# Seven block products for part of the first matmul in the last five passes of an attention and feed-forward kernel, with a re-ordered start

## Chip, cores, metric

One core of a Trainium2 chip. The metric is device time in microseconds, from runs of the whole program. The engines are PE (matmuls), PEld (its weight loads), DVE (vector), ACT (scalar), POOL, and SP, which issues most transfers (all but two in the trace of before).

## The reference, cut

```python
# per batch of 8, head of 8; seq 576, head_dim 64
q_s = softmax over head_dim of q;  k_s = softmax over seq of k
x = q_s @ (k_s.T @ v)                      # heads side by side: (8, 576, 512)
xn = (x - mean) / sqrt(var + 1e-6) * g_ln
out = x + relu(xn @ w_ch1) @ w_ch2         # 512 -> 2048 -> 512
```

The kernel works in nine passes: eight with 512 tokens of one batch each, and a ninth with the 64 tokens left of each batch. g_ln and the mean are worked into w1 ("centring"); the division by the deviation comes at the end.

## The kernel before: the parts concerned

The kernel is a list of tasks, each with an engine, an estimated duration, what it reads and writes, and a priority class. A small simulation of the engines at build time puts them into one fixed order per engine; at run time each engine works through its list strictly in that order. An order that rests on a transfer that lands later than estimated makes the engine stand (DVE for 0.87 us, up to 22.35 us, in the trace of before).

The first matmul of a pass makes 16 blocks of 128 hidden units from four blocks of x:

```python
for n, m in enumerate(order):                        # 16 blocks
    for ko in range(k0, KO1):                        # 4 matmuls 512 wide
        nc.tensor.matmul(bank[gi], w1_sb[:, ko, m*P:m*P+P], xt[:, ko], ...)
    relu_evac(m, bank[gi], (bk, gi), eng(n))         # PSUM -> fp16 hT
    if split and n in (HK, KO2 - 1):
        sums(0 if n == HK else 4)                    # sums of hT for the second matmul
```

Cutting both operands of a matmul into 2 x 2 blocks gives eight block products; with sums and differences of blocks as operands, seven are enough, an eighth fewer multiplications for some additions (in the trace of before an undisturbed matmul of a pass took 12.23 us in seven products and 13.81 us plain). The second matmul was already in seven block products, save in the first pass. DVE makes the sums that this needs (`S` of hT, `T` of w2) and adds up the products as they come out of PSUM (`cp`, `ot`).

The start loads w1 in four column blocks, converts each on ACT or DVE, takes its column mean through a matmul with a matrix of ones, and subtracts it on DVE:

```python
on_act = ((1,), (0, 1, 3), (1,), (1, 3))[blk]
...
after = state["kve"] if blk == 1 and (kp or ko not in on_act) else ()
if blk == 2:
    after = (state["nm"],) if ko in on_act else state["ev"][1]
```

The attention of a later batch goes beside the matmuls: loads of q, k and v; exponentials on ACT (`eq`, `ek`); copy of v to fp16 (`vb`); key-value products (PE, evicted as `kve`); a transposition of `eq` by DMA; and the x products, evicted on ACT to `xsT`, which the next first matmul reads.

The softmax here doesn't subtract the row's maximum and nothing guards it: scores larger than these inputs give would overflow.

## Time and profile before

| | before |
|---|---|
| median of 3 timed runs | 279.06 us (278.26 to 279.4) |
| profiled run, span | 277.7 us, 275.9 us |
| first matmuls of batch 1, 2 and 4 start at (PE timeline) | 52.25, 80.10, 135.89 us |
| end of PE's last matmul | 272.08 us |

The page of the profile gives busy time and the chain of work that ended last, followed back from the end. The timeline lists instructions in time, with the idle time ahead of them and what ended it in brackets. "Stretches" give length, then busy time of PE, PEld, DVE, ACT and POOL with instruction counts, then the granted PE clock, the DMA share (in this view it can exceed 1) and GB/s. The prediction shows the lines of before.

### The profile page before, as it was taken

To read this page: it belongs to the slowest core of one execution; us is meant where nothing else is said; L and a number is where in the kernel's file an instruction comes from. 1 tells how busy PE (TensorE), PEld (TensorE's weight loads), DVE (VectorE), ACT (ScalarE), POOL (GpSimd) and SP (SyncE) were. 2 spreads that over 40 slices of the span, in tenths; PEclk is the share of its full clock that TensorE was granted. 3 is DMA by queue.
4 is the path that set the end of the run, shared out by engine and by line. 5 is a ranking of instruction groups with operands and counts; after the bars stand their busy time and mean duration, and the time that the engine had idled before them with its cause. 6 is when DMAs were issued, how large, how long until landed. Compare 5 with 4: busy or idle time off the path is not lost.

```text
span 275.9 us, 5670 instructions
## 1 busy us (share of the span) xinstructions
PE 268.4 (97%) x2324; PEld 163.7 (59%) x2324; DVE 198.5 (72%) x412; ACT 168.2 (61%) x274; POOL 1.7 (1%) x12
## 2 busy tenths in 40 slices
PE   8988999999999999999999999999999999999994
PEld 3433445446864587458745874578457845874583
DVE  1788998998769767966697669766976764742562
ACT  4678966788598693659466856685664076016500
POOL 2000000000000000000000000000000000000000
PEclk9999999999999999999999999999999999999999
DMA  7999999799989994499659965796544450022004
GB/s 257 361 386 387 388 388 233 184 330 256 319 265 187 280 334 48 143 216 389 75 153 185 395 100 154 160 394 124 154 86 77 78 154 0 0 64 90 1 4 152
DMA packets 55874, 54.83 MB, mean 199 GB/s; under 512 B 34596, under 2 KB 35112, under 8 KB 55848
## 3 DMA queue, kind: packets, MB, share of 16 engines
q1 hardware_dynamic: 55696, 54.34, 69.6%
q8 instruction: 18, 0.29, 0.4%
q10 hardware_dynamic: 152, 0.13, 0.1%
q14 instruction: 8, 0.07, 0.1%
HBM read 36.70 MB, written 9.44 MB: 167 GB/s over the span
## 4 chain that ended last, share of the span: by engine, by line
PE 91%; DMA 4%; SPq 1%; ACT 1%; DVE 1%; issue 0%
PE pg L575 43%; PE pg L654 35%; PE pg L717 5%; DMA stg<-in_v_dram 4%; PE pa L391 2%; PE pa L422 2%; PE pa L654 1%; PE pa L575 1%; SPq L238 1%; PE pa L288 1%; PE pg L553 1%; ACT hT L538 1%; PE pa L445 0%; PE pa L519 0%; DVE vb L377 0%; ACT w_sb L271 0%
## 5 line engine op out<-in xcount | busy, mean ns | idle before, releaser
L538 ACT ACTIVATE hT<-pg 128x512 f16<-128x512 f32 x134 | 78.8, 598 | 65.2 <-PE pg L575 64.8
L575 PE MATMUL pg<-xsT,w_sb 128*128 128x512 f16 x488 | 108.4, 379 | 0.8 <-ACT hT L538 0.8
L575 PEld LDWEIGHTS <-w_sb 128*128 128x128 f16 x568 | 54.8, 98 | 65.9 <-DVE w_sb L294 1.6
L654 PEld LDWEIGHTS <-S 128*128 128x128 f16 x512 | 49.6, 98 | 6.3 <-issue 0.4
L654 PE MATMUL pg<-T,S 128*128 128x256 f16 x368 | 41.9, 273 | 0.0
L654 PEld LDWEIGHTS <-hT 128*128 128x128 f16 x384 | 37.2, 98 | 7.8 <-issue 2.2
L591 DVE TENSOR_TENSOR S<-hT 128x1024 f16<-128x1024 f16 x32 | 21.8, 681 | 26.5 <-ACT hT L538 26.5
L664 DVE SCALAR_TENSOR_TENSOR cp<-pg,st,x 128x256 f32<-128x256 f32 x46 | 20.2, 479 | 14.2 <-PE pg L654 13.7
L664 DVE SCALAR_TENSOR_TENSOR ot<-pg,st,cp 128x256 f32<-128x256 f32 x47 | 20.5, 477 | 12.2 <-PE pg L654 12.0
L654 PE MATMUL pg<-w_sb,hT 128*128 128x256 f16 x248 | 29.2, 273 | 0.0
L527 DVE BATCH_NORM_STATS2 bst<-x 128x6 f32<-128x512 f16 x36 | 23.9, 666 | 4.8 <-DMA x<-xsT 4.8
L342 DVE TENSOR_REDUCE zq<-eq 128x18 f32<-128x1152 bf16 x16 | 21.5, 1344 | 4.7 <-ACT eq L340 4.7
L340 ACT ACTIVATE eq<-stg 128x1152 bf16<-128x1152 f32 x16 | 18.7, 1170 | 7.3 <-DMA stg<-in_q_dram 7.2
L346 DVE TENSOR_TENSOR eq<-eq,rzq 128x1152 bf16<-128x1152 bf16 x16 | 21.6, 1352 | 0.3
L370 ACT ACTIVATE ek<-stg 128x1152 bf16<-128x1152 f32 x16 | 18.7, 1170 | 3.0 <-DMA stg<-in_k_dram 3.0
L380 ACT CAST vb<-stg 128x1152 f16<-128x1152 f32 x15 | 17.6, 1174 | 4.4 <-DMA stg<-in_v_dram 4.3
L435 ACT CAST xsT<-pa 128x512 f16<-128x512 f32 x31 | 16.0, 592 | 3.0 <-PE pa L422 3.0
L654 PE MATMUL pg<-w_sb,S 128*128 128x256 f16 x128 | 15.3, 273 | 0.0
L717 PE MATMUL pg<-w_sb,hT 128*128 128x512 f16 x64 | 14.8, 380 | 0.0
L654 PE MATMUL pg<-T,hT 128*128 128x256 f16 x120 | 14.4, 273 | 0.0
L575 PE MATMUL pg<-xT,w_sb 128*128 128x512 f16 x64 | 14.0, 379 | 0.0
L740 PE MATMUL pg<-zero 128*128 128x512 f16 x33 | 10.6, 481 | 1.2 <-DVE zero L223 1.2
(71 smaller groups left out, 162.6 us busy)
## 6 DMA issues: line engine op xcount, KB each, us to landing
stg<-in_q_dram SPq DMA_DIRECT2D x16, 576.0 KB, 5.3
stg<-in_k_dram SPq DMA_DIRECT2D x16, 576.0 KB, 7.2
stg<-in_v_dram SPq DMA_DIRECT2D x16, 576.0 KB, 9.0
out_dram<-ot SPq DMA_DIRECT2D x33, 256.0 KB, 3.7
stg<-in_moe_w_ch_dram SPq DMA_DIRECT2D x16, 512.0 KB, 10.8
out_dram<-ot SPq DMA_DIRECT2D x1, 512.0 KB, 2.8
out_dram<-ot SPq DMA_DIRECT2D x1, 128.0 KB, 2.7
out_dram<-ot ACTq DMA_DIRECT2D x1, 128.0 KB, 2.2
```

Source lines behind the costliest of these rows:

```text
L340: plan.add("ACT", act_t(QW), lambda: nc.scalar.activation(e.rearrange("p j (s d) -> p s j d", s=2), sv(s), AF.Exp), r=sk(s), w=[("eq", u, ...
L342: plan.add("DVE", dve_t(QW), lambda: nc.vector.reduce_sum(zq[:, hf], eh, axis=AX.X), r=[("eq", u, hf)], w=[("zq", hf)], cls=qcls, after=sums_)
L346: plan.add("DVE", dve_t(QW), lambda: nc.vector.tensor_tensor(eh, eh, rzq[:, hf].to_broadcast([P, 2 * JT, D]), op=ALU.mult), r=[("rzq", hf) ...
L370: plan.add("ACT", act_t(QW), lambda: nc.scalar.activation(ek[u][:, hf].rearrange("p j (s d) -> p s j d", s=2), sv(s), AF.Exp), r=sk(s), w= ...
L380: plan.add("ACT", act_t(QW), lambda: nc.scalar.copy(vd, va), r=sk(s), w=[("vb", u, hf, i) for i in range(2)], cls=cls, slack=late, after=t ...
L527: plan.add("DVE", dve_t(512), lambda j=j: nc.vector.bn_stats(bst[:, j, :], x[:, j, :]), r=[(xk, j)], w=[("bst", j)], cls=cls, slack=2.0 if ...
L538: nc.scalar.activation(hT[:, m, :], bank, AF.Relu)
L575: nc.tensor.matmul(bank[gi], w1_sb[:, ko, m * P : m * P + P], xt[:, ko], start=(ko == 0), stop=(ko == KO1 - 1))
L591: plan.add("DVE", dve_t(256 * n, 2), lambda: nc.vector.tensor_tensor(S[i][:, ks], a, b, op=op), r=r, w=sk(i), cls=0.3 if k0 else 0.45)
L654: nc.tensor.matmul(g[i][0], fa(k, i), fb(k), start=(first and k == 0 and (i == 0 or g[0][1] != g[1][1])), stop=(last and k == HK - 1), ski ...
L664: nc.vector.scalar_tensor_tensor(dst[:, i, :], in0=g[i][0], scalar=sti[:, 4, 2 * t0 + i : 2 * t0 + i + 1], in1=src[:, i, :], op0=ALU.mult, ...
L717: nc.tensor.matmul(pg[gis[j]], hT[:, kk, j * P : j * P + P], w2_sb[:, kk, :], start=(kk == 0), stop=(kk == KO2 - 1))
```

## The change

Its intent: the first matmul too in seven block products, for as many row groups of w1 as the other engines can carry, one in batches 4 to 6 and two in batch 7 and the ninth pass; a start whose order fits the landing of its loads; and v rows 66 wide instead of 65, so that each starts on 4 bytes. Cut to its core:

```diff
-    vb = [sb([P, 2, JT, 2, VW], FP16, f"vb{i}") for i in range(2)]
+    vb = [sb([P, 2, JT, 2, VW + 1], FP16, f"vb{i}") for i in range(2)]
-        on_act = ((1,), (0, 1, 3), (1,), (1, 3))[blk]
+        on_act = ((0, 1), (0, 1), (1,), (1, 3))[blk]
-                after = state["kve"] if blk == 1 and (kp or ko not in on_act) else ()
+                after = state["kve"] if blk == 1 and ko else ()
-                    after = (state["nm"],) if ko in on_act else state["ev"][1]
+                    after = (state["nm"],) if ko in on_act else (state["subs"],) if kp else state["ev"][1]
+        for k0, k1 in ((0, 2), (2, 4)) if blk == 0 else ((0, 4),):   # centring in two halves
-            queries(1, lq, kves[:1])
+            queries(1, lq, kves)
-            keys(1, lk)
+            keys(1, lk, (state["nm"],))
 ... (load estimates, slack, keys of hT by half)
+    UNITS = {c: (1,) for c in (4, 5, 6)}
+    UNITS[7] = UNITS[8] = (0, 1)
+    def w1_sums(n, before): ...      # 4 DVE sums of w1 quarters -> WS[n]
+    def x_sums(c): ...               # 4 DVE differences of x quarters -> TX
+            def product(self, a, b, g, first, last): ...   # 4 matmuls 256 wide
+            def copy(self, g, n): ...                      # ACT: PSUM -> fp32 SBUF
+            def end(self, g, m0, t, n=None): ...           # ACT ReLU, or DVE add + max
+            u.product("11", "11", 0, True, False);  u.copy(0, 0)
+            u.product("12", "21", 1, True, True);   u.end(1, 0, 0, 0)
+            u.product("S2", "T2", 0, False, False); u.copy(0, 1)
+            u.product("S1", "T1", 2, True, False);  u.copy(2, 2)
+            u.product("S3", "T3", 0, False, False); u.end(0, HK, 1, 2)
+            u.product("S4", "22", 2, False, True);  u.end(2, 0, 1, 1)
+            u.product("22", "T4", 0, False, True);  u.end(0, HK, 0)
```

More of the change, by code (lines that the diff above doesn't have):

```diff
@@ L260, in load_w1 @@
             load(stg[s][:, :1024].rearrange("p (a n) -> p a n", a=2),
-                 w1_src[:, 2 * kp : 2 * kp + 2, blk * 512 : blk * 512 + 512], sk(s), 0.524 if blk or kp else 0.72)
+                 w1_src[:, 2 * kp : 2 * kp + 2, blk * 512 : blk * 512 + 512], sk(s), 0.524 + (0.4 if (blk, kp) == (2, 0) else 0))
             for a in range(2):
                 ko = 2 * kp + a
-                after = state["kve"] if blk == 1 and (kp or ko not in on_act) else ()
+                after = state["kve"] if blk == 1 and ko else ()
                 if blk == 2:
-                    after = (state["nm"],) if ko in on_act else state["ev"][1]
+                    after = (state["nm"],) if ko in on_act else (state["subs"],) if kp else state["ev"][1]
                 dst = w1_sb[:, ko, blk * 512 : blk * 512 + 512]
@@ L285, in centre_w1, with f @@
         wk = [("w1", blk, ko) for ko in range(KO1)]
-        def f():
-            for ko in range(KO1):
-                nc.tensor.matmul(bank, ones, w1_sb[:, ko, cs], start=(ko == 0), stop=(ko == KO1 - 1))
-        plan.add("PE", 0.216 * KO1, f, r=wk + ["ones"], w=[bk], cls=0)
+        for k0, k1 in ((0, 2), (2, 4)) if blk == 0 else ((0, 4),):
+            def f(k0=k0, k1=k1):
+                for ko in range(k0, k1):
+                    nc.tensor.matmul(bank, ones, w1_sb[:, ko, cs], start=(ko == 0), stop=(ko == KO1 - 1))
+            plan.add("PE", 0.216 * (k1 - k0), f, r=wk[k0:k1] + ["ones"], w=[bk], cls=0)
         state["nm"] = plan.add("ACT", act_t(512), lambda: nc.scalar.copy(nm, bank), r=[bk], w=["nm"], cls=-0.5)
@@ L302, in centre_w1 @@
         sub(0, 4, 0, 1)
-        sub(0, 4, 1, 4)
+        state["subs"] = sub(0, 4, 1, 4)
     def load_w2(k0, eng="DVE"):
@@ L367, in pe_t_evac, with keys @@
             plan.add("ACT", act_t(128), lambda: nc.scalar.copy(et[:, hf, 8], v16[1][:, 0]), r=[("pa", tb[1])], w=[("eqT", u, 2)], cls=0)
-        def keys(hf, s):
+        def keys(hf, s, exps=exps):
             plan.add("ACT", act_t(QW), lambda: nc.scalar.activation(
@@ L391, in f @@
                                 nc.tensor.matmul(pa[ab[n][e]][c0 : c0 + D, :VW], ek[u][r0 : r0 + R, hf, j, c0 : c0 + D],
-                                                 vb[u][r0 : r0 + R, hf, j, i, :], start=(j == 0), stop=(j == JT - 1))
+                                                 vb[u][r0 : r0 + R, hf, j, i, :VW], start=(j == 0), stop=(j == JT - 1))
             ids = []
@@ L395, in kv @@
             plan.add("PE", 0.1 + 0.42 * len(hs), f, r=[("ek", u, h) for h in hs] + [("vb", u, h, i) for h in hs for i in range(2)],
-                     w=[("pa", a) for x in ab for a in x], cls=0, slack=SLACK if steady else 0.2, after=kvs)
+                     w=[("pa", a) for x in ab for a in x], cls=0, slack=SLACK if steady else 0.2 if b else 0.0, after=kvs)
             for n, h in enumerate(hs):
@@ L456, in attn @@
         if kind == "first":
-            lq, lk, lv = [load_half(b, t, 0, x) for t, x in ((q, 0), (k, 0), (v, 0))]
+            lq, lk, lv = [load_half(b, t, 0, x) for t, x in ((q, 0), (k, 0), (v, 0.2))]
             queries(0, lq)
@@ L541, in relu_evac @@
         if eng == "ACT":
-            plan.add("ACT", act_t(512), fa, r=[bk], w=[("hT", m)], cls=0)
+            plan.add("ACT", act_t(512), fa, r=[bk], w=[("hT", m, 0), ("hT", m, 1)], cls=0)
         else:
-            plan.add("DVE", dve_t(512), fd, r=[bk], w=[("hT", m)], cls=0)
+            plan.add("DVE", dve_t(512), fd, r=[bk], w=[("hT", m, 0), ("hT", m, 1)], cls=0)
     def mm1_open(gis):
@@ L580, in mm1, with sums @@
         return ids
-    def sums(k0):
+    def sums(k0, seven=False):
         n = 4
@@ L587, in sums @@
         h12, h22 = hT[:, kh, 0:256], hT[:, kh, 256:512]
-        lo, hi = [("hT", k0 + i) for i in range(n)], [("hT", HK + k0 + i) for i in range(n)]
+        lo, hi = [[("hT", k + i, t) for i in range(n) for t in range(2)] for k in (k0, HK + k0)]
         sk = lambda i: [("S", i, k0 + j) for j in range(n)]
         def tt(i, a, b, op, r):
-            plan.add("DVE", dve_t(256 * n, 2), lambda: nc.vector.tensor_tensor(S[i][:, ks], a, b, op=op), r=r, w=sk(i), cls=0.3 if k0 else 0.45)
+            plan.add("DVE", dve_t(256 * n, 2), lambda: nc.vector.tensor_tensor(S[i][:, ks], a, b, op=op), r=r, w=sk(i),
+                     cls=(-0.25 if i < 2 else -0.1) if seven else 0.3 if k0 else 0.45)
         tt(0, h21, h22, ALU.add, lo + hi)
@@ L634, in mm2_split @@
         rk = lambda t0: [(stk, "r", 2 * t0), (stk, "r", 2 * t0 + 1)]
-        hk = lambda k0: [("hT", k0 + k) for k in range(HK)]
+        hk = lambda k0, t: [("hT", k0 + k, t) for k in range(HK)]
         skey = lambda i: [("S", i, k) for k in range(HK)]
@@ L639, in mm2_split @@
         h = lambda k, t0, i: hT[:, k, 256 * t0 + i * P : 256 * t0 + i * P + P]
-        A = {"11": (lambda k, i: h(k, 0, i), hk(0)), "12": (lambda k, i: h(HK + k, 0, i), hk(HK)),
-             "22": (lambda k, i: h(HK + k, 1, i), hk(HK))}
+        A = {"11": (lambda k, i: h(k, 0, i), hk(0, 0)), "12": (lambda k, i: h(HK + k, 0, i), hk(HK, 0)),
+             "22": (lambda k, i: h(HK + k, 1, i), hk(HK, 1))}
         for i in range(4):
@@ L647, in mm2_split, with product @@
             Bm[f"T{i + 1}"] = ((lambda k, i=i: T[i][:, k, :]), tkey(i))
-        def product(a, b, g, first, last):
+        def product(a, b, g, first, last, after=()):
             (fa, ka), (fb, kb) = A[a], Bm[b]
@@ L656, in f @@
                                          skip_group_check=True)
-                plan.add("PE", 0.1093 * len(ks), f, r=[ka[k] for k in ks] + [kb[k] for k in ks], w=[g[i][1]])
+                n = plan.add("PE", 0.1093 * len(ks), f, r=[ka[k] for k in ks] + [kb[k] for k in ks], w=[g[i][1]], after=after)
+            return n
         gk = lambda g: [g[0][1], g[1][1]] if g[0][1] != g[1][1] else [g[0][1]]
@@ L686, in mm2_split @@
         add_x(2, gb, 1, 256)
-        product("S3", "T3", ga, False, False)
+        n = product("S3", "T3", ga, False, False)
         state["stats"] = (final(o2, 1, ga, 2, 1),)
@@ L691, in mm2_split @@
                      r=[("ot", o2, 1)], mb=0.26, land=2.0, cls=0)
-        product("S4", "22", gb, False, True)
+        product("S4", "22", gb, False, True, (n,) if c == B else ())
         final(o1, 1, gb, 1, 0)
@@ L718, in f @@
                                          start=(kk == 0), stop=(kk == KO2 - 1))
-                i = plan.add("PE", 0.864, f, r=[("hT", kk) for kk in range(k0, k0 + 4)] + [("w2", kk) for kk in range(k0, k0 + 4)], w=[("pg", gis[j])])
+                i = plan.add("PE", 0.864, f, r=[("hT", kk, t) for kk in range(k0, k0 + 4) for t in range(2)] + [("w2", kk) for kk in range(k0, k0 + 4)], w=[("pg", gis[j])])
                 if j == 0:
@@ L744, in warm, with w1_sums, tt @@
         return plan.add("PE", 0.43 * n, lambda: zeros(pg[3], True)(n), r=["zero"], w=[("pg", 3)], cls=0)
+    UNITS = {c: (1,) for c in (4, 5, 6)}
+    UNITS[7] = UNITS[8] = (0, 1)
+    WS = [ek[0].bitcast(FP16).rearrange("p a j c -> p (a j c)")[:, :2048].rearrange("p (i k n) -> p i k n", i=4, k=2),
+          sb([P, 4, 2, 256], FP16, "WS1")]
+    WSK = [[("ek", 0, 0), ("ek", 0, 1)], []]
+    def w1_sums(n, before):
+        lo, hi = slice(256 * n, 256 * n + 256), slice(1024 + 256 * n, 1024 + 256 * n + 256)
+        a11, a12, a21, a22 = w1_sb[:, 0:2, lo], w1_sb[:, 2:4, lo], w1_sb[:, 0:2, hi], w1_sb[:, 2:4, hi]
+        def tt(i, a, b, op, r=()):
+            plan.add("DVE", dve_t(512, 2), lambda: nc.vector.tensor_tensor(WS[n][:, i], a, b, op=op),
+                     r=list(r) + [("w1c", m0 + 2 * n + j, k) for m0 in (0, HK) for j in range(2) for k in range(2)], w=WSK[n] + [("WS", n, i)], cls=0.8, after=before)
+        tt(0, a21, a22, ALU.add)
+        tt(1, WS[n][:, 0], a11, ALU.subtract, [("WS", n, 0)])
+        tt(3, a12, WS[n][:, 1], ALU.subtract, [("WS", n, 1)])
+        tt(2, a11, a21, ALU.subtract)
@@ new lines, in x_parts @@
+    def x_parts(c):
+        xt = (xsT[c % 2] if c < B else xT8).rearrange("p (j k) t -> p k j t", j=J)
+        xkeys = XK(c % 2) if c < B else [("xT8", b, i) for b in range(B) for i in range(2)]
+        if c < B - 1:
+            return xt, xkeys, x8.rearrange("p j (k n) -> p j k n", k=2), [("x8", j) for j in range(J)]
+        tx = ek[1].bitcast(FP16).rearrange("p a j c -> p (a j c)")[:, :2048].rearrange("p (i k n) -> p i k n", i=4, k=2)
+        return xt, xkeys, tx, [("ek", 1, 0), ("ek", 1, 1)]
@@ new lines, in x_sums, with tt @@
+    def x_sums(c):
+        xt, xkeys, TX, tk = x_parts(c)
+        b11, b12, b21, b22 = [xt[:, 2 * k : 2 * k + 2, 2 * t : 2 * t + 2, :] for k in range(2) for t in range(2)]
+        T4 = lambda i: TX[:, i].rearrange("p k (j t) -> p k j t", j=2)
+        def tt(i, a, b, r=()):
+            plan.add("DVE", dve_t(512, 2), lambda: nc.vector.tensor_tensor(T4(i), a, b, op=ALU.subtract),
+                     r=xkeys + list(r), w=tk + [("TX", i)], cls=0.2)
+        tt(0, b12, b11)
+        tt(1, b22, T4(0), [("TX", 0)])
+        tt(2, b22, b12)
+        tt(3, b21, T4(1), [("TX", 1)])
@@ new lines, in mm1_seven, with __init__, product, f @@
+    def mm1_seven(c):
+        last = c >= B - 1
+        units = UNITS[c]
+        xt, xkeys, TX, tk = x_parts(c)
+        bufs = [(t, (n, i)) for n, ts in (("pg", pg), ("pa", pa)) for i, t in enumerate(ts)]
+        raw = lambda k0, m0: (lambda n, k, m: w1_sb[:, k0 + k, (m0 + 2 * n + m) * P : (m0 + 2 * n + m) * P + P])
+        A = {"11": raw(0, 0), "12": raw(2, 0), "22": raw(2, HK)}
+        for i in range(4):
+            A[f"S{i + 1}"] = lambda n, k, m, i=i: WS[n][:, i, k, m * P : m * P + P]
+        Bm = {"11": (lambda k: xt[:, k, 0:2, :], xkeys), "21": (lambda k: xt[:, 2 + k, 0:2, :], xkeys),
+              "22": (lambda k: xt[:, 2 + k, 2:4, :], xkeys)}
+        for i in range(4):
+            Bm[f"T{i + 1}"] = ((lambda k, i=i: TX[:, i, k, :]), [("TX", i)])
+        ids = []
+        class Unit:
+            def __init__(self, n):
+                self.n = n
+                if last:
+                    self.g = [bufs[(3 * n + i) % 8] for i in range(3)]
+                    self.cp = [(stg[3 * n + i][:, :512], sk(3 * n + i)) for i in range(3)]
+                else:
+                    self.g = [(pa[i], ("pa", i)) for i in [nxt("pa", 4) for _ in range(3)]]
+                    self.cp = [(cp[i], [("cp", i)]) for i in range(3)]
+            def product(self, a, b, g, first, last):
+                fa, (fb, kb) = A[a], Bm[b]
+                bank, bk = self.g[g]
+                def f():
+                    for i in range(2):
+                        for k in range(2):
+                            nc.tensor.matmul(bank[:, 256 * i : 256 * i + 256], fa(self.n, k, i), fb(k),
+                                             start=(first and i == 0 and k == 0), stop=(last and k == 1), skip_group_check=True)
+                ids.append(plan.add("PE", 0.437, f, r=kb + ([("WS", self.n, int(a[1]) - 1)] if a[0] == "S" else []), w=[bk]))
+            def copy(self, g, n):
+                bank, bk = self.g[g]
+                plan.add("ACT", act_t(512), lambda: nc.scalar.copy(self.cp[n][0], bank), r=[bk], w=self.cp[n][1], cls=-0.3)
+            def end(self, g, m0, t, n=None):
+                bank, bk = self.g[g]
+                bank = bank.rearrange("p (i n) -> p i n", i=2)
+                m = m0 + 2 * self.n
+                h = hT[:, m : m + 2, 256 * t : 256 * t + 256]
+                w = [("hT", m, t), ("hT", m + 1, t)]
+                if n is None:
+                    plan.add("ACT", act_t(512), lambda: nc.scalar.activation(h, bank, AF.Relu), r=[bk], w=w, cls=-0.2)
+                    return
+                cp_, ck = self.cp[n]
+                plan.add("DVE", dve_t(512), lambda: nc.vector.tensor_tensor(h, bank, cp_.rearrange("p (i n) -> p i n", i=2), op=ALU.add),
+                         r=[bk] + ck, w=w, cls=-0.3)
+                if t == 0 or not last:
+                    plan.add("DVE", dve_t(512, 4), lambda: nc.vector.tensor_scalar_max(h, in0=h, scalar1=0.0), r=w, w=w, cls=-0.2)
+                else:
+                    plan.add("ACT", act_t(512), lambda: nc.scalar.activation(h, h, AF.Relu), r=w, w=w, cls=-0.1)
+        def direct(m):
+            if last and m >= HK:
+                gi = nxt("pa", 4)
+                bank, bk = pa[gi], ("pa", gi)
+            else:
+                gi = nxt("pg", 4)
+                bank, bk = pg[gi], ("pg", gi)
+            def f():
+                for ko in range(KO1):
+                    nc.tensor.matmul(bank, w1_sb[:, ko, m * P : m * P + P], xt[:, ko], start=(ko == 0), stop=(ko == KO1 - 1))
+            ids.append(plan.add("PE", 0.864, f, r=xkeys, w=[bk]))
+            relu_evac(m, bank, bk, "ACT")
+        for n0 in (0, 2):
+            for n in (n0, n0 + 1):
+                for m in [m0 + 2 * n + i for i in range(2) for m0 in (0, HK)] if n not in units else ():
+                    direct(m)
+            us = [Unit(n) for n in (n0, n0 + 1) if n in units]
+            for u in us:
+                u.product("11", "11", 0, True, False)
+                u.copy(0, 0)
+                u.product("12", "21", 1, True, True)
+                u.end(1, 0, 0, 0)
+            for u in us:
+                u.product("S2", "T2", 0, False, False)
+                u.copy(0, 1)
+                u.product("S1", "T1", 2, True, False)
+                u.copy(2, 2)
+            for u in us:
+                u.product("S3", "T3", 0, False, False)
+                u.end(0, HK, 1, 2)
+                u.product("S4", "22", 2, False, True)
+                u.end(2, 0, 1, 1)
+            for u in us:
+                u.product("22", "T4", 0, False, True)
+                u.end(0, HK, 0)
+            sums(2 * n0, last)
+        return ids
@@ L777 @@
             state["tok"] = tokens(b, 0.7 if b > 1 else 0.35, stats=state["stats"])
+        rstd = state.get("rstd")
+        if b == min(UNITS) - 1:
+            w1_sums(1, before)
+        if b == B - 2:
+            w1_sums(0, before)
+        if b in UNITS:
+            x_sums(b)
+        ids = mm1_seven(b) if b in UNITS else mm1(b, b > 0, () if b else opened)
         if b == B - 1:
-            tokens(8, 0.7, stats=state["stats"])
-        rstd = state.get("rstd")
-        ids = mm1(b, b > 0, () if b else opened)
+            tokens(8, 0.9, stats=state["stats"])
+            x_sums(8)
         if b == 0:
@@ L794 @@
         before = (ids[-1], rstd)
-    mm1(8, True)
+    mm1_seven(8)
     mm2_split(8)
```

## The prediction

> **What bounds the kernel now.** I read the head of the page first, then the chain of work that ended last in order of time, then the stretches between the starts of its stages, then the groups. On the page:
>
> ```profile
> span 275.9 us, 5670 instructions
> PE 268.4 (97%) x2324; PEld 163.7 (59%) x2324; DVE 198.5 (72%) x412; ACT 168.2 (61%) x274; POOL 1.7 (1%) x12
> PE 91%; DMA 4%; SPq 1%; ACT 1%; DVE 1%; issue 0%
> ```
>
> PE is 97% busy, and, which says more, 91% of the chain that set the end is PE, mostly one matmul behind another (line 575 is the first matmul, 654 the second one, already in seven block products). The chain in order of time gives the stage lengths:
>
> ```profile
> 20.49 0.59 ACT cp L290
> 21.07 0.64 ACT w_sb L271
> 21.71 1.47 ACT hT L538 x3
> 23.18 0.04 issue
> 23.23 1.90 PE pg L575 x8
> ...
> 219.95 13.81 PE pg L575 x64
> 233.76 12.23 PE pg L654 x112
> 245.99 13.81 PE pg L575 x64
> ```
>
> An undisturbed first matmul is 13.81 us for 64 matmuls 512 wide, 215.8 ns each. An undisturbed second one is 12.23 us for 112 matmuls 256 wide, 109.2 ns each. From 23.23 us on the chain hardly leaves PE. So matmul time taken away there is time saved, if nothing new makes PE wait. Ahead of 23.23 us there are a DMA wait and a hole. The timeline of DVE in the hole:
>
> ```profile
> 20.99 0.49 DVE L274 TENSOR_SCALAR w_sb<-stg,g_sb 128x512 f16<-128x512 f32 x1 [0.67 <-DMA stg<-in_moe_w_ch_dram]
> 22.35 0.49 DVE L274 TENSOR_SCALAR w_sb<-stg,g_sb 128x512 f16<-128x512 f32 x1 [0.87 <-DMA stg<-in_moe_w_ch_dram]
> 22.75 1.28 DVE L294 TENSOR_TENSOR w_sb<-w_sb,cp 128x512 f16<-128x512 f16 x2
> ```
>
> The subtraction that releases column block 1 of w1 (line 294, at 22.75) has had its operand since ACT wrote it at 21.08, but in DVE's fixed order it stands behind two conversions of block 2 whose transfers had not landed. PE began its next matmuls at 23.23. That is an ordering fault, and the diff aims at it.
>
> Room on the other engines, one row per batch (batches 3 to 8, the last with the tail):
>
> ```profile
> 108.19:136.05 27.86, 27.86 (x266) 18.00 (x264) 20.44 (x44) 18.78 (x30) 0.00 (x0) 1.00 0.81 206
> 136.05:164.03 27.98, 27.98 (x265) 17.97 (x264) 20.86 (x45) 18.77 (x30) 0.00 (x0) 1.00 0.79 205
> 164.03:192.09 28.06, 28.02 (x266) 18.00 (x264) 21.30 (x46) 18.78 (x30) 0.00 (x0) 1.00 0.74 205
> 192.09:219.95 27.86, 27.86 (x266) 17.98 (x264) 22.05 (x49) 12.32 (x24) 0.00 (x0) 1.00 0.45 98
> 219.95:245.99 26.04, 26.04 (x178) 17.23 (x176) 15.43 (x34) 10.11 (x20) 0.00 (x0) 1.00 0.15 42
> 245.99:275.90 29.91, 26.08 (x177) 17.03 (x174) 12.62 (x24) 9.54 (x16) 0.00 (x0) 1.00 0.23 71
> ```
>
> After the length come busy PE, weight loads, DVE, ACT, POOL. PE fills every batch; DVE has 6 to 7 us free in batches 4 to 6 and 10 or more in the last two; the clock is full.
>
> [...] seven products instead of eight keep nearly all of their 12.5%. [...] (a 512-element sum for w2 took 414 to 416 ns, a 1024-element one 690) and for PSUM (a 512-element eviction took 682 ns)[...]. [...] The v rows are 65 fp16 wide, 130 bytes[...]; the cast into them took 753 ns for 576 elements[...], where the aligned fp32-to-fp16 cast of w2 took 690 ns for 1024[...]. [...] whether 66-wide rows help is open.
>
> **The change part by part.**
>
> *Matmuls.* A row group is four blocks of 128 hidden units. Plain, it takes 4 x 4 = 16 matmuls of 512: 13.81 / 4 = 3.45 us. In seven products of 2 x 2 matmuls of 256 it takes 28 x 109.2 ns = 3.06 us. Saved 0.39 us. There is one such group in each of batches 4, 5 and 6 and two in each of passes 7 and 8 (the last pass is that of the ninth tokens): seven groups, 7 x 0.395 = 2.8 us, all of it on the PE chain. Weight loads rise from 16 to 28 a group at 98 ns each, under the 109 ns spacing, as in the second matmul now.
>
> *ACT.* A plain group has four evictions of 0.60 us. The new one has three copies and one ReLU of the same 512 elements: the same 2.4 us. In the last two passes two ReLUs a group are added; ACT has over 15 us free there.
>
> *DVE.* A group gets three additions from PSUM (0.68 us each, as the eviction row) and three maxima on fp16 [...], 2.9 us; in the last two passes only one maximum, 2.3 us. Each such pass needs four differences of x (4 x 0.41 = 1.7 us, done in the batch before), and each group once four sums of w1 (1.7 us, in batches 3 and 6). New DVE sums: batch 3, 20.4 + 3.3 = 23.7 of 27.9; batch 4, 20.9 + 4.6 = 25.5 of 27.6; batch 5, 21.3 + 4.6 = 25.9 of 27.7; batch 6, 22.1 + 4.6 + 1.7 = 28.4 of 27.5, so nearly 1 us must move to its neighbours; batch 7, 15.4 + 4.6 + 1.7 = 21.7 of 25.2; the last, 12.6 + 4.6 = 17.2. It fits, at 92 to 100% in three batches.
>
> *PSUM and order.* Within one group a product that adds to a bank must wait for the copy out of it: about 0.6 us and a hand-over, against 0.44 us of the product between. The plan can put plain matmuls of another group there, and in the last passes two groups alternate. I charge 0.05 to 0.1 us a group, 0.4 us in all, for waits that the plan's model misses.
>
> *Start.* Conversions of w1 move between ACT and DVE (block 0 to ACT, block 1 to DVE), the first value product is no longer parted by a conversion waiting on a transfer, the centring of block 0 opens after two of its four matmuls' data, and the late half of block 2 is put behind the subtraction of block 1. The clear part is the hole: the subtraction takes about 0.42 us for its first part, so from 21.08 PE could begin near 21.6 to 22.3 instead of 23.23: 0.9 to 1.6 us. The cast of v may lose another 0.3 us ahead of the first matmul at 17.24, but ACT's own half of v ends at 16.56, so little of that counts. Against it: DMA is busy at 98% or more from 17 to 80 us, so what waits for transfers there cannot move up, and ACT, which works in order, evicted x for batch 2 only at 78.74, behind a key conversion whose load landed at 77.67; the first matmul of batch 2 at 80.17 started just as that eviction went on. I let 0.9 us come through.
>
> Sum: 2.8 - 0.4 + 0.9 = 3.3 us, so 279.06 - 3.3 = 275.8 us.
>
> **Rivals.** *DVE becomes the bound in batches 4 to 6.* For it: the sums above, and that DVE worked without a break over the first 13 us of batch 4, just where the new additions fall. They push the query normalisation, its transpose and the x products later by up to 3 us. Against it: x products of batch 5 began at 151.73 and are needed at 164.03, and the first 10 us of slack take this in. If it wins, PE waits 0.5 to 1 us in each of three batches and the result is 277 to 278 us. *The start gain is hidden by transfers.* For it the DMA shares; against it, PE runs unbroken from 23.23 on and the waits there are of order. If it wins fully, 276.7 us. *The start gain comes whole*, 1.6 us, and the plan's waits are nil: 274.7 us. *The groups' waits for PSUM copies are not filled*: up to 0.4 us at two places in each of seven groups, 5 us, which would turn the change into a loss of 2 us less the start gain; the plan sees these waits and has other matmuls ready, so I give it little.
>
> **Range and chances.** 274.5 to 277.3 us holds most of this. Over 2% faster would be under 273.5, 5.6 us, which needs twice the matmul saving or a start gain that no row above shows: 5%. Slower by 2% needs the unfilled waits and a lost start together: 1%. Within 2%: 94%.
>
> **What would show it.** The chain of the profile after should have first matmuls of 13.4 us of PE time in batches 4 to 6 and 13.0 in the last two, with no DVE or ACT pieces in it; the stretches should show DVE near 25.5 us in batches 4 and 5; PE's idle time after 25 us should stay below 1 us; the first matmuls after the hole should start near 22.3; and the v cast should show 753 ns or about 450. I am wrong if DVE releases PE again and again in batches 4 to 7, if matmuls 256 wide with w1 as weights come at over 115 ns, or if the start of batch 1 (52.41) does not move up by 0.5 to 1.5 us.

In the sums for DVE the ground of one term is: a group's 2.9 us (2.3 in the last two passes) are three additions of 0.68 us, as the eviction of 682 ns, and 0.9 us for three maxima (0.3 for one). The trace of before has no such maximum; in the changed kernel one took 287 ns (line 841). That seven products keep nearly all of their eighth is in the chain: 28 x 109.2 ns against 16 x 215.8 ns is 11.4% less. What wider v rows would give no trace had shown. The 0.3 us, and the "about 450" ns at the end, can stand only as an estimate: 576 elements on the line through the sums' 415 ns for 512 and 690 for 1024, which is also what the cast of w2 took for 1024, make 0.45 us.

## The result and the profile after

275.25 us, median of 4 runs (274.09 to 275.85), beside 278.96 us for before: faster, by less than 2%. The ratio is 0.9864 (95% interval 0.9825 to 0.9904). A ratio is the mean time of one kernel's fast runs over that of the other's of the same rounds, so not quite the ratio of these medians. Predicted were 275.8 us and a gain of 3.3 us; measured were 3.7. Line numbers move: 854 and 819 are the plain and the seven-product matmuls of the new routine, 576 the old first matmul, 656 the second.

The head of the page of the kernel after, and its chain by engine:

```profile
span 273.1 us, 5912 instructions
PE 264.3 (97%) x2403; PEld 171.3 (63%) x2403; DVE 224.0 (82%) x474; ACT 169.6 (62%) x282; POOL 1.7 (1%) x12
PE 74%; DMA 15%; DVE 4%; ACT 3%; SPq 2%; issue 2%
```

PE busy fell by 4.1 us, partly because fewer filler matmuls run in the start (28 instead of 33). DVE rose by 25.5 us and PE stayed at 97%. The chain now leaves PE more often: DMA has 15% of it, against 4%. That is where to look for the start. The share is not lost time: PE's named waits after 25 us sum to 0.85 us (0.41, 0.23 and 0.21), but at each of them the chain goes back to the work that released PE. The groups of the new work (line, engine, operation, output and inputs, count, busy us, mean ns, idle before):

```profile
L838 DVE TENSOR_TENSOR hT<-pa,cp 128x512 f16<-128x512 f32 x9 | 5.9, 682 | 0.0
L841 DVE TENSOR_SCALAR hT<-hT 128x512 f16<-128x512 f16 x13 | 3.5, 287 | 0.2
L825 ACT COPY cp<-pa 128x512 f32<-128x512 f32 x9 | 5.0, 586 | 0.2 <-PE pa L819 0.2
L378 DVE CAST vb<-stg 128x576 f16<-128x576 f32 x1 | 0.8, 754 | 0.0
```

The additions took 682 ns each, as the prediction has them, and the maxima 287 ns: 3 x 0.682 + 3 x 0.287 = 2.9 us a group, the prediction's sum. The v cast on DVE took 754 ns, 753 before: the wider rows did nothing for it. PE's timeline in batch 4 holds the one wait of the new routine:

```profile
141.93 0.60 PE L819 MATMUL pa<-xsT,WS 128*128 128x256 f16 x4
142.36 1.03 PE L854 MATMUL pg<-xsT,w_sb 128*128 128x512 f16 x4
...
145.76 0.60 PE L819 MATMUL pa<-x,w_sb 128*128 128x256 f16 x4 [0.21 <-DVE hT L838]
```

The next row starts 0.43 to 0.44 us after four matmuls 256 wide (141.93 to 142.36): 109 ns each, as expected. Plain matmuls stand between the products of the group, so that the copies out of PSUM are hidden. Only the seventh product waited, 0.21 us, for a DVE addition.

The stretches of 27.6, 27.6 and 27.4 us from the start of batch 4:

```profile
136.00:163.60 27.60, 27.39 (x272) 18.58 (x271) 24.92 (x55) 17.08 (x30) 0.00 (x0) 1.00 0.76 208
163.60:191.20 27.60, 27.60 (x274) 18.73 (x272) 25.01 (x54) 19.48 (x34) 0.00 (x0) 1.00 0.81 208
191.20:218.60 27.40, 27.40 (x279) 19.30 (x278) 24.22 (x56) 13.30 (x25) 0.00 (x0) 1.00 0.47 99
```

DVE is at 88 to 91%, PE has next to no gap. PE's first row of batch 4 and its last row, before:

```profile
135.89 9.78 PE L575 MATMUL pg<-xsT,w_sb 128*128 128x512 f16 x44
...
271.04 1.04 PE L654 MATMUL pa<-T,hT 128*128 128x256 f16 x8
```

and after:

```profile
135.83 3.65 PE L854 MATMUL pg<-xsT,w_sb 128*128 128x512 f16 x16
...
268.25 1.04 PE L656 MATMUL pa<-T,hT 128*128 128x256 f16 x8
```

From the first matmul of batch 4 to PE's end (start and length of the last row) the kernel before took 272.08 - 135.89 = 136.19 us, this one 269.29 - 135.83 = 133.46 us: 2.73 us less, for seven groups at an expected 0.395, 2.77.

The start is another story. The old hole is gone, but a new one stands at block 2. DVE in the kernel after:

```profile
26.29 0.69 DVE L311 CAST w_sb<-stg 128x1024 f16<-128x1024 f32 x1 [0.87 <-DMA stg<-in_moe_w_ch_dram]
27.02 0.43 DVE L607 TENSOR_TENSOR T<-w_sb 128x512 f16<-128x512 f16 x1
27.36 1.29 DVE L295 TENSOR_TENSOR w_sb<-w_sb,cp 128x512 f16<-128x512 f16 x2
```

A conversion of w2 stands ahead of the subtraction, waiting for its load; PE waited 0.41 us for the subtraction. The first matmul of batch 1 still began 0.58 us earlier (51.67 instead of 52.25), but that of batch 2 only 0.13 us earlier (79.97 instead of 80.10). The chain in order of time shows the loss:

```profile
69.72 7.88 DMA stg<-in_k_dram
...
77.62 0.03 ACT ek L371
77.64 1.04 issue
78.69 1.06 ACT xsT L436 x2
...
79.79 0.25 PE pa L446 x6
80.04 9.73 PE pg L576 x44
```

ACT evicts x for batch 2 only after a key exponential of batch 3 whose load landed at 77.6. So I had two theories to test. P: the products are the whole gain, and the start gain is lost again ahead of batch 2 by an engine's fixed order. S: about 1 us of the start does come through, which would explain why the timed runs differ by 3.7 us where the trace shows 2.8 (span 275.9 to 273.1). Later ones: T, full DMA queues hand every gain of the start back; and D, DVE is about to become the bound.

### The profile page after: what moved, and what is told of

Read it like the earlier page. It is cut to its first block, busy times and chain, and to the rows that moved or that the text cites. A ratio compares the mean times of both kernels' runs of the same rounds, so it can differ in the third digit from the quotient of the medians.

```text
span 273.1 us, 5912 instructions
## 1 busy us (share of the span) xinstructions
PE 264.3 (97%) x2403; PEld 171.3 (63%) x2403; DVE 224.0 (82%) x474; ACT 169.6 (62%) x282; POOL 1.7 (1%) x12
## 4 chain that ended last, share of the span: by engine, by line
PE 74%; DMA 15%; DVE 4%; ACT 3%; SPq 2%; issue 2%
PE pg L656 26%; PE pg L576 15%; PE pg L854 11%; DMA stg<-in_moe_w_ch_dram 7%; PE pg L720 5%; PE pg L819 4%; PE pa L819 3%; DMA stg<-in_k_dram 3%; DMA x<-xsT 3%; PE pa L854 3%; DMA stg<-in_v_dram 2%; PE pa L392 2%; SPq L238 1%; PE pa L576 1%; PE pa L656 1%
## 5 line engine op out<-in xcount | busy, mean ns | idle before, releaser
L539 ACT ACTIVATE hT<-pg 128x512 f16<-128x512 f32 x98 | 57.8, 599 | 34.2 <-PE pg L854 20.6
L576 PE MATMUL pg<-xsT,w_sb 128*128 128x512 f16 x232 | 51.9, 379 | 0.4 <-DVE w_sb L295 0.4
L656 PE MATMUL pg<-T,S 128*128 128x256 f16 x368 | 43.5, 273 | 0.0
L576 PEld LDWEIGHTS <-w_sb 128*128 128x128 f16 x248 | 23.7, 98 | 29.3 <-DVE w_sb L295 1.2
L854 PE MATMUL pg<-xsT,w_sb 128*128 128x512 f16 x160 | 38.3, 379 | 0.0
L854 PEld LDWEIGHTS <-w_sb 128*128 128x128 f16 x208 | 20.0, 98 | 17.6 <-issue 0.2
```

What stands on the lines that cost most here:

```text
L539: nc.scalar.activation(hT[:, m, :], bank, AF.Relu)
L576: nc.tensor.matmul(bank[gi], w1_sb[:, ko, m * P : m * P + P], xt[:, ko], start=(ko == 0), stop=(ko == KO1 - 1))
L656: nc.tensor.matmul(g[i][0], fa(k, i), fb(k), start=(first and k == 0 and (i == 0 or g[0][1] != g[1][1])), stop=(last and k == HK - 1), ski ...
L854: nc.tensor.matmul(bank, w1_sb[:, ko, m * P : m * P + P], xt[:, ko], start=(ko == 0), stop=(ko == KO1 - 1))
```

## The experiments

Twelve runs follow, the first of the changed kernel itself. Each edit reaches the chip through the plan, which can move other instructions too: PE's list is that of the changed kernel in e3, e4b, e5b and e10; in e4, e8 and e9 it changed with the edit, in e1, e2 and e7 it must. In the table, starts come from PE's timeline of the one profiled run, times from 6 runs. Where a kernel's own profile and its timed runs differ, it is because the same kernel's runs spread by 1 to 3 us. e0, e1, e2 and e4, and later e8 to e10, ran on one chip, e4b, e5b, e6 and e3 on a second, e7 on a third; each group beside runs of the kernel before.

### e0: the changed kernel again

> The changed kernel once more, unaltered, as the yardstick for the runs beside it and for a second trace. Its first trace puts batches 4 to the end 2.7 us under before (what the seven groups should give) and the start of batch 2 only 0.1 us earlier, yet the timed runs differed by 3.7 us. Theory P (the products are the whole gain, the start gain is swallowed in batch 1): 2.6 to 3.0 us under before. Rival S (about 1 us of the start does come through in the timed runs): 3.5 to 4.0 us under before.

Measured: 274.43 us against 278.01, ratio 0.9876 (0.984 to 0.9912). Batch 1 starts at 51.30, batch 2 at 79.82, batch 4 to the end takes 133.04 us. The timed difference, 3.5 us, lies where S begins; the interval (2.4 to 4.4 us) holds both theories.

### e1: the products with the old start

The edit takes back every hunk of the start and of the v rows, for instance:

```diff
-        on_act = ((0, 1), (0, 1), (1,), (1, 3))[blk]
+        on_act = ((1,), (0, 1, 3), (1,), (1, 3))[blk]
-            queries(1, lq, kves)
+            queries(1, lq, kves[:1])
```

> The seven products with the old start: all edits of the loading and centring of w1, of the first attention and of the v rows taken back. Theory P: 2.6 to 3.0 us under before, within 0.3 us of the changed kernel. Rival S: only the 2.7 us of the matmuls remain and the changed kernel is about 1 us faster than this.

Measured: 275.30 us, ratio 0.9896 (0.9865 to 0.9927), so 2.9 us under before. From batch 4 to the end 133.50 us, as with the changed kernel. Theory P's number. The difference from e0, 0.6 us in the means, is within the noise.

### e2: the start without the products

The same hunks put onto the old kernel, with the padded rows.

> The old kernel with the new start and the padded v rows, without the seven products. Theory P: within 0.3 us of before, with mm1 of batch 1 starting some 0.7 us earlier and mm1 of batch 2 at the old time, held by ACT, which stands behind a key load that has not landed. Rival S: about 1 us under before.

Measured: 277.93 us against 278.01, ratio 1.0003 (0.9966 to 1.004): nothing; S's 1 us lies at the interval's edge (0.34%, 0.9 us). In the profile, batch 1 starts at 51.41, 0.84 us earlier, and batch 2 at 81.01, later than before; from batch 4 to the end 136.20 us, as before (136.19). ACT stood at the query load of batch 3 until 74.17, in front of an eviction that PE waited for.

### e4: keys behind the evictions of x

```diff
-                r=sk(s), w=[("ek", u, hf)], cls=cls, slack=late, after=exps)
+                r=sk(s), w=[("ek", u, hf)], cls=cls, slack=late,
+                after=tuple(exps) + (tuple(state["ev"][-1]) if b == 3 else ()))
```

> The changed kernel with one order edge added: the two key exponentials of batch 3 on ACT go behind the four evictions of x of batch 2. If the start gain is lost because those evictions wait behind a key load (theory P), the first matmul of batch 2 begins at 79.4 to 79.6 us instead of 80.04 and the whole is 0.4 to 0.6 us faster than the changed kernel. If the transfers themselves are the bound there (rival T: everything in that stretch is held by the full DMA queues), the wait turns up elsewhere, in the value products of batch 3 or the next transposition, and nothing is gained.

Measured: 275.73 us, ratio 0.9912 (0.9883 to 0.9942), 1.1 us slower in the means than e0. Batch 2 starts at 79.45, 27.89 us after batch 1: without a gap, as theory P wanted. But the plan moved the value products of batch 3 from 89.70 to 92.50 us, and PE waited 0.57, 0.47 and 0.27 us between 97 and 103 us. P's account of the loss is right, its forecast of a gain was wrong.

### e4b: only the second keys behind them

The same edge with `b == 3 and hf`; PE's order is that of the changed kernel.

> The changed kernel; of batch 3 only the second key exponential goes behind the four evictions of x of batch 2, PE's order stays as it was. The last run moved both keys: its batch 2 started at 79.4 us without a gap, but the value products of batch 3 then went 3 us later and PE waited 1.3 us in that batch. If the loss of the start gain is ACT's order and not the transfers (theory P), this starts the first matmul of batch 2 at 79.3 to 79.6 us, keeps the value products of batch 3 near 89.2 us, and is 0.3 to 0.6 us faster than the changed kernel. If the transfers hold that stretch (rival T), batch 2 starts early but PE waits again before batch 4 and the time stays within 0.2 us of the changed kernel.

Measured: 275.16 us, ratio 0.9896 (0.9869 to 0.9922). Batch 2 starts at 79.83, again with no gap after batch 1 (51.97), and no wait follows before batch 4. But the start itself was 0.3 us later in this run, and the time is no better. Against an interval of 0.3%, a gain of 0.3 to 0.6 us can't be confirmed.

### e5b: that, and w2's first conversion behind the subtraction

```diff
-            r=sk(s), w=[("w2", k0), ("w2", k0 + 1)])
+            r=sk(s), w=[("w2", k0), ("w2", k0 + 1)], after=(state["subs2"],) if k0 == 0 else ())
```

> The edge of the run before, and the first conversion of w2 on DVE put behind the subtraction of column block 2 of w1, so that DVE no longer stands at a w2 load in front of it (0.87 us of idle time, 0.4 us of it passed on to PE in the changed kernel at 27.8 us). Theory P: the wait at 27.8 us goes, the first matmul of batch 1 starts 0.3 to 0.5 us earlier, and 0.2 to 0.5 us of it comes through: 0.6 to 1.0 us faster than the changed kernel, the fastest so far. Rival T: batch 2 starts when its transfers let it, no faster than the run before.

Measured: 274.83 us, ratio 0.9887 (0.9861 to 0.9913), the same as e4b; theory P's 0.6 to 1.0 us under the changed kernel did not come. The wait at 27.8 us is gone and batch 1 starts at 51.42. Then ACT stood at the first query load of batch 3 until 73.84, PE waited 0.53 us for the eviction behind it, and batch 2 started at 80.21. The gain of the start was taken away at the same place by another load.

### e6: two groups in batch 6 (a failed experiment)

```diff
-    UNITS[7] = UNITS[8] = (0, 1)
+    UNITS[6] = UNITS[7] = UNITS[8] = (0, 1)
... (and the sums of w1 for the first group get priority class 0.2 instead of 0.8)
```

> A second row group in seven products in batch 6: PE has 0.39 us less, DVE 2.9 us more work there. The prediction's sums say that DVE is at 28.4 us of 27.5 in batch 6 already with one group and moves the rest to its neighbours. If DVE is close to being the bound (rival D), PE waits on it in batches 6 and 7 and the run is 0.3 to 2 us slower than the changed kernel, with DVE named in PE's idle time. If DVE still has room (theory P's simplest form), it is 0.3 to 0.4 us faster.

Measured: 283.25 us, ratio 1.0191 (1.0159 to 1.0223), and the result is wrong (relative error 0.17). The fault is mine: in batches 4 to 6 a group takes three of four PSUM banks, so two of the second group's three banks are still open in the first; that is read from the code, not tested. PE waited 5.85 us at one place. The run tells nothing on DVE's room, since the shared banks add waits of their own; e8 was made in its place.

### e3: v rows 65 wide

```diff
-    vb = [sb([P, 2, JT, 2, VW + 1], FP16, f"vb{i}") for i in range(2)]
+    vb = [sb([P, 2, JT, 2, VW], FP16, f"vb{i}") for i in range(2)]
```

> The changed kernel with the v rows 65 wide again, every instruction in the same order. The one v cast on DVE took 754 ns in the changed kernel and 753 before, so both theories expect the same: within 0.3 us of the changed kernel. A rival left is that the products that read the v rows go faster with aligned rows; then the 36 products of a half take longer here than the 0.41 us of the changed kernel.

Measured: 275.74 us, ratio 0.9928 (0.9893 to 0.9963). Every engine's list is that of the changed kernel. The value products took 195 ns each against 194. The only difference is in the v casts on ACT. Without the padding:

```profile
L381 ACT CAST vb<-stg 128x1152 f16<-128x1152 f32 x15 | 17.6, 1173 | 2.4 <-DMA stg<-in_v_dram 2.4
```

and in the changed kernel:

```profile
L381 ACT CAST vb<-stg 128x1152 f16<-128x1152 f32 x15 | 17.4, 1158 | 2.7 <-DMA stg<-in_v_dram 2.7
```

15 ns of 1173, 0.2 us of ACT in all; the other traces agree (1150 to 1159 ns with the padding, 1173 and 1174 without). This run is 1.3 us slower than e0 in the means, on another chip; its profile has ACT standing at the query load of batch 3 until 75.20 and batch 2 starting at 82.04. From batch 4 to the end it took 133.05 us, as e0. With the same lists and the load's landing 2.2 us later, this is the chance of the transfers more likely than the padding, but the interval leaves it open.

### e8: the differences of x computed twice

```diff
-        tt(0, b12, b11) ... tt(3, b21, T4(1), [("TX", 1)])
+        for _ in range(2):
+            tt(0, b12, b11) ... tt(3, b21, T4(1), [("TX", 1)])
```

> The changed kernel with the four differences of x computed twice over (the second time the same values): 1.7 us more work on DVE in each of batches 3 to 7, nothing else. This doubles one of the costs that the change adds. If DVE still has room (theory P: PE alone sets the length of batches 4 to 8), the time stays within 0.5 us of the changed kernel and PE's idle time in batches 4 to 8 within 0.5 us. If DVE is at its limit there (rival D, my sums had it at 92 to 100%), the extra work comes out at the end: 2 us or more slower, with DVE named as what PE waits for.

Measured: 280.01 us, ratio 1.0058 (1.0007 to 1.0109): 5.7 us slower in the means than e0 on the same chip (5.1 us by the two ratios), for 1.7 us more DVE work in each of five batches. So the number that rival D forecast came, and DVE is named in PE's waits. PE's waits after batch 4 in its timeline:

```profile
185.53 1.03 PE L656 MATMUL pg<-T,S 128*128 128x256 f16 x8 [1.75 <-DVE cp L667]
216.51 0.60 PE L656 MATMUL pg<-T,S 128*128 128x256 f16 x4 [1.80 <-DVE cp L667]
```

The waits sum to 3.55 us, yet from batch 4 to the end it took 140.04 us, 6.6 us more than the changed kernel. Short stretches after the first wait show the rest (the PE clock is third from the end):

```profile
186.50:187.50 1.00, 1.00 (x15) 0.83 (x15) 0.90 (x4) 1.00 (x3) 0.00 (x0) 0.80 1.06 401
187.50:188.50 1.00, 1.00 (x7) 0.67 (x6) 0.67 (x2) 1.00 (x4) 0.00 (x0) 0.50 1.06 394
188.50:189.50 1.00, 1.00 (x7) 0.67 (x6) 1.00 (x4) 1.00 (x2) 0.00 (x0) 0.50 1.06 394
189.50:190.50 1.00, 1.00 (x6) 0.72 (x5) 0.28 (x1) 0.54 (x2) 0.00 (x0) 0.50 1.49 345
```

In the next microsecond the clock was 0.99. So about 1.6 us after PE resumed at 185.5 the granted clock fell to half for some 3.4 us: 0.20 + 3 x 0.50 = 1.7 us of PE time lost in these rows. The second wait did the same, from about 1.3 us after it (0.94 from 216.5 to 218, 0.50 to 221, 0.88 to 222). 3.55 + 2 x 1.7 = 7.0 us, near the 6.6. A wait of 1.30 us in e3 (up to 78.12 us) left the mean clock of that span at 1.000. The times agree: the three runs of e8 with mean clock 0.999 to 1.0 took 278.9 to 279.6 us, those with 0.980 to 0.992 took 280.4 to 283.0.

Whether DVE had run out of time is not shown by this, for the edit did more than add work: the plan changed the orders of PE, DVE and ACT too. Ahead of the first wait DVE was no busier than in the changed kernel (18.33 us of 164 to 184, against 18.81 there), and the eviction that PE waited for ran at 184.60 us (184.63 there). What differed is what PE had to do meanwhile. In the changed kernel PE worked on the first matmul of batch 6 from 184.18 us. Here DVE's second query normalisation ran at 174.76 us instead of 169.16, and the x products of batch 6 came later. In the changed kernel and in this run:

```profile
178.95 0.63 PE L423 MATMUL pa<-eqT,kve 64*64 64x512 bf16 x8
183.15 0.63 PE L423 MATMUL pa<-eqT,kve 64*64 64x512 bf16 x8
```

Their evictions on ACT began at 184.47 us instead of 179.39; until then ACT, in its new order, had stood 5.42 us for the statistics. So no matmul of batch 6 was ready to fill the wait. More DVE work cost 5 us in these orders; orders that keep x early were not tried.

### e9: the queries behind batch 2's evictions

```diff
-            queries(hf, lq[hf])
+            queries(hf, lq[hf], first=() if b != 3 else
+                    tuple(state["ev"][-1]) if hf else tuple(state["kve_ids"]))
```

> The changed kernel; of batch 3 the first query exponential on ACT goes behind the two evictions of the key-value products of batch 2, and the second behind the four evictions of x of batch 2. In the traces so far the first matmul of batch 2 starts late whenever the first query load of batch 3 lands later than about 72.9 us, because ACT stands at it. Theory Q (that load, in ACT's fixed order, decides the start of batch 2): PE has no gap from the start of batch 1 to that of batch 2 (27.9 us apart), whenever the load lands. Rival T: batch 3 pays it back, as when both keys were moved, with PE waits between 90 and 103 us and a time 0.5 to 1.5 us above the changed kernel.

Measured: 274.75 us, ratio 0.9871 (0.9841 to 0.99), equal to the changed kernel. ACT's timeline:

```profile
72.77 0.71 ACT L406 ACTIVATE kve<-pa,rz 128x64 f16<-128x64 f32 x2 [3.42 <-DVE rz L401]
73.38 1.15 ACT L341 ACTIVATE eq<-stg 128x1152 bf16<-128x1152 f32 x1
75.16 1.16 ACT L371 ACTIVATE ek<-stg 128x1152 bf16<-128x1152 f32 x1 [0.62 <-DMA stg<-in_k_dram]
76.23 2.03 ACT L436 CAST xsT<-pa 128x512 f16<-128x512 f32 x4
```

x is evicted 2.5 us earlier than in the changed kernel, and batch 2 starts at 79.44, 27.85 us after batch 1 with no gap: theory Q as to the place. Then PE waited 0.33 and 0.42 us for DVE evictions in the first matmul of batch 3, and batch 4 started at 136.25, later than in the changed kernel (135.83). The lead was paid back in batch 3, as rival T has it, but by evictions on DVE and not by a transfer, and the time is not the 0.5 to 1.5 us longer that T forecast. The query load had landed by 73.38 us in this run, so a later landing was not put to the test.

### e10: the query loads earlier

```diff
-            gate[0] = state["eqT"]
+            gate[0] = state["eqT"] if b != 3 else ()
         lq = [load_half(b, q, hf) for hf in range(2)]
+        if b == 3:
+            gate[0] = state["eqT"]
```

> The changed kernel with the two query loads of batch 3 let go ahead of the transposition of batch 2's queries in the DMA queue, instead of behind it. Theory Q: they land well ahead of 72 us, ACT doesn't stand at them, the first matmul of batch 2 starts 27.9 us after that of batch 1 with no gap, and the time is 0.3 to 0.7 us under the changed kernel, with less spread between its runs. Rival T (the queues are full, what is moved ahead pushes something else back): the transposition lands later, PE waits for the x products of batch 2 by way of it, and the time is the same or worse.

Measured: 275.52 us, ratio 0.9894 (0.9864 to 0.9923). The query exponentials of batch 3 ran at 69.27, 3.9 us earlier than in the changed kernel, and batch 2 started at 79.50, 27.90 us after batch 1. PE then waited 0.25 us in batch 2 for the transposition of batch 3's queries, and batch 4 started at 135.83, exactly as in the changed kernel: of the lead of 0.47 us, 0.25 went in that wait, the rest I did not trace. Again Q at the place and no gain in the whole. The runs spread by 1.1 us, those of e0 by 1.8.

### e7: seven products in the last two passes only

```diff
-    UNITS = {c: (1,) for c in (4, 5, 6)}
-    UNITS[7] = UNITS[8] = (0, 1)
+    UNITS = {}
+    UNITS[7] = UNITS[8] = (0, 1)
```

(and both sets of w1 sums in batch 6)

> The changed kernel without the seven products in batches 4, 5 and 6, so four groups instead of seven, all in the last two passes. Theory P (0.395 us of PE a group, and nothing else): from the first matmul of batch 4 to the end the trace takes 3 x 0.395 = 1.2 us more than the 133.3 us of the changed kernel, 134.5 us, and the time is 1.2 us longer, 276 us beside a before of 278.5. Rival D (the groups in batches 4 to 6 cost in DVE waits what they save in matmuls): no longer than the changed kernel, as taking them out relieves DVE by 4.6 us a batch.

Measured: 276.78 us against 278.11, ratio 0.9956 (0.9934 to 0.9978), a gain of 1.2 us where the full change had 3.4 to 3.8 by its two ratios. From batch 4 to the end 134.24 us: 0.78 us more than the first trace of the changed kernel and 1.20 us more than the second (e0, 133.04). So the three groups of batches 4 to 6 bring two thirds to all of their matmul saving of 1.2 us; 0 to 0.4 us goes back in waits, of which the first trace shows 0.21 us, at 145.76. In the timed runs the difference is larger than 1.2 us, within wide intervals. Both speak against D's form here: the three groups pay.

### What the starts say together

| kernel | batch 1 | first query exp. of batch 3 | batch 2 | batch 4 | batch 4 to end |
|---|---|---|---|---|---|
| before | 52.25 | 72.36 | 80.10 | 135.89 | 136.19 |
| after | 51.67 | 73.13 | 79.97 | 135.83 | 133.46 |
| e0 | 51.30 | 72.97 | 79.82 | 135.69 | 133.04 |
| e1 | 51.82 | 73.55 | 80.59 | 136.32 | 133.50 |
| e2 | 51.41 | 74.17 | 81.01 | 136.87 | 136.20 |
| e3 | 52.03 | 75.20 | 82.04 | 137.90 | 133.05 |
| e5b | 51.42 | 73.84 | 80.21 | 136.12 | 133.76 |
| e10 | 51.60 | 69.27 | 79.50 | 135.83 | 133.73 |

All in us, from the timelines. With ACT's order as it was, batch 2 starts at 79.8 to 80.1 us where that exponential runs by 73.2 us (there the key load behind it, landing near 77.6, comes last), and the later the later it runs from 73.5 us on: 73.55, 74.17 and 75.20 go with 80.59, 81.01 and 82.04. When batch 1 began matters little. The last column splits by the number of seven-product groups: 136.2 without, 133.0 to 133.8 with seven.

## Why the prediction was right

*The matmul saving.* 7 x 0.395 = 2.8 us: confirmed. The trace gives 2.73 us from batch 4 on, and with the edited kernels of the table 2.4 to 3.2. The step of 256-wide matmuls at 109 ns holds with w1 and its sums as weights. e1 and e2 part it from the start: the products alone gain 2.9 us (2.0 to 3.7), the start alone nothing (0.9 us faster to 1.1 us slower).

*Waits of the groups.* Charged 0.05 to 0.1 us a group. One wait of 0.21 us is named in the profile; e7 puts the price of the three groups in batches 4 to 6 at 0 to 0.4 us, as the one or the other trace of the changed kernel is taken, and the last passes show no wait. On the whole the first trace falls short of 2.77 us by 0.04, so the charge of 0.4 us was too high there; e0's trace gains 3.15 us, more than the matmuls explain, which I did not trace.

*DVE.* Predicted near 25.5 us in batches 4 and 5, measured 24.9 and 25.0. I gave batch 6 28.4 us and a spill to its neighbours; measured 24.2. One of the four w1 sums ran in batch 5 already (at 183.95), and busy time counts the overlap of neighbouring instructions once, where I added their durations; the rest of the difference I did not trace. The 0.68 us that the prediction gives for the additions from PSUM is of a tensor-scalar eviction (682 ns, line 540 of before); the new additions, which are tensor-tensor, took 682 ns as well. The rival that DVE becomes the bound did not win. e8 shows that 1.7 us more a batch can cost 5 us, but as the orders moved with it, it doesn't show how much room DVE has. The forecast's own path for this rival, later x products, is the one that e8 took.

*The start.* This step was mis-sized. "I let 0.9 us come through" came from the hole at 23.23 us. The hole was mended as described, and batch 1 began 0.6 to 1.0 us earlier, but a hole of the same kind opened at 27.8 us, and by batch 2 the two traces of the changed kernel hold 0.1 and 0.3 us. e2, the start alone, gains nothing in time. The objection that the prediction raised itself, ACT standing at a load in front of the evictions of x, was what happened, with the query load as well as the key load. Its premise that loads there "cannot move up" since DMA is full was too strong: the share of 98% is a mean by stages (from 45 to 52 us it was 0.79), and in e10 the query exponentials ran 3.9 us earlier, once the loads were let go earlier.

*The v rows.* Left open, with little of an estimated 0.3 us counted; the DVE cast did not change (754 ns, 753 before).

*The signs named beforehand.* PE's idle time after 25 us is 0.85 us, under the 1 us; there is no hole left near 22 us (12 matmuls run from 19.90 us, the next at 22.75, where PE had started block 1 again only at 23.23); batch 1 moved up by 0.58 us (0.5 to 1.5 asked). DVE pieces do stand in the chain of batch 4, between 134.7 and 145.7 us, through the one wait of 0.21 us; from 145.76 us to 269.30 the chain is PE alone. The 13.4 and 13.0 us of a first matmul can't be read off, since the new order mixes it with the second matmul of the batch before.

*The sum.* 3.3 us predicted, 3.7 and 3.5 measured, of which the two traces of the changed kernel show 2.7 and 3.2 from batch 4 on. The trace of before is of a run of 277.7 us, faster than the medians of 277.9 to 279.1 of its timed runs, so part of the remainder is the choice of that run. That the total came out so near is in part luck: without the 0.9 us of the start, which the traces don't show, the prediction would have said 2.4 us. Whether up to 0.6 us of the start comes through on average (e0 against e1) stays open: the intervals are wider than that.

No experiment beats the changed kernel beyond its interval; e9 and e5b are equal to it.

## What to carry to other kernels

Here, where PE sets the end without gaps, a block scheme with fewer products paid its count of matmuls almost to the tenth of a microsecond. Other ready matmuls filled the waits for PSUM copies; in e8, where none were ready, two waits cost 7 us with the clock's fall. So after such a change look at what PE has to do while it waits for the sums, and not only at how busy the engine is that makes them. A gain ahead of a stretch in which in-order engines stand at loads is not a gain yet (here 0.58 us at batch 1 was 0.13 us at batch 2): follow it to the next stage's start, and the one after, before counting it. Don't let an engine's fixed order put next stage's work on an unlanded load in front of this stage's eviction; and when that is mended, look for the wait one stage further on.
